# Cosformer attention into a quick-GELU MoE layer: two numerators of batch 0 in one PSUM tile, with early denominators and a different idle stream

## The chip, the cores and the metric

The kernel runs on one core of one Trainium2 chip. The metric is the device time of one execution in microseconds; 292.02 us is the median of three runs of the kernel before.

## The reference

Linear attention with cosine weights, for 8 batches, 8 heads, 576 positions and a head size of 64; then an expert layer over all 4608 tokens.

```python
def phi(x, c, s):
    r = np.maximum(x, 0.0)
    return np.concatenate([r * c, r * s], axis=-1)
q_p = phi(q, cos_w, sin_w)
k_p = phi(k, cos_w, sin_w)
kv = np.einsum('bhsf,bhsd->bhfd', k_p, v)
z = np.sum(k_p, axis=2)
num = np.einsum('bhsf,bhfd->bhsd', q_p, kv)
den = np.einsum('bhsf,bhf->bhs', q_p, z)[..., None] + 1e-06
return (num / den).astype(np.float32)
...
h = x @ w_in
g = h * (1.0 / (1.0 + np.exp(-1.702 * h)))
return (g @ w_out).astype(np.float32)
```

x is the attention's output with the heads side by side, 4608 x 512; w_in is 512 x 2048, w_out 2048 x 512.

## The kernel before

The order of the instructions on every engine is that of the source: the kernel is written under a manual schedule, and the framework only adds the waits. A wait is put where an instruction touches a tile that an instruction of another engine wrote or read.

Batch 0 has a lead-in of its own, since nothing can hide it. Its order on TensorE, with the lines of the profile:

- idle(12) (L346) multiplies a tile of zeros, warm, while the first loads run. Idle matmuls also stand between the next steps.
- trig (L140 on ScalarE, L142 on VectorE and for one slice on GpSimd) makes kr, the weighted relu of k, in nine slices j of 64 positions. ksum(j) (L218) multiplies each slice with sel, so that the PSUM tile z holds the sum over positions for each head; ksum_evac (L222) copies it to column 64 of kvs. The second half of k lands later than the first, so slices 3 to 8 come later.
- trig makes qn from q likewise; qturn_pe(c) (L171) transposes two slices of it at a time, a chunk c of 128 positions, and qevac(c) (L179 ScalarE, L181 VectorE) copies it to qT.
- kv_mm(0, 2) and kv_mm(2, 4) (L207) make kv for heads 0 to 3 and 4 to 7, and kv_evac (L212) copies each to columns 0 to 63 of kvs.
- den_early(0) (L244) makes the denominators of chunk 0 from column 64 of kvs alone, before kv is there; inv_of (L236, L238) adds 1e-6 and takes the reciprocal.
- num_mm(c) (L230) makes the numerators of chunk c, with 65 columns for a head so that the last is the denominator; num_div(c) (L254) multiplies with the reciprocal into xn; xturn_mm(c) (L274) transposes xn back into free columns of the same PSUM tile, and xturn_evac (L280, ScalarE) copies that into xT. Chunk 4 has 64 positions and goes through a DMA transpose (L285).
- part(c, ...) (mm1_part, L295) multiplies w_in with chunk c of xT for one of the first four slices of the hidden layer, so that the expert layer starts before all of xT is there. Then gelu (L300), the other slices, and mm2 (L332) with w_out.

Two PSUM pools matter. pmm has four tiles of one bank ("mm"): idle, z, the transposes of q, the early denominators and the hidden slices take them in turn. pat has two tiles of two banks ("at"): the two halves of kv, then one chunk's numerators after the other. So num_mm(2) takes the tile of chunk 0, and waits until xturn_evac(0, 0) has read it; num_mm(3) takes that of chunk 1.

Batches 1 to 7 are pipelined: their loads, trig, transposes and kv run beside the expert layer of the batch before.

Of the kernel before, what the change touches and what calls it, by code (L numbers as in the profile page):

```python
# [9 lines left out]
F32 = mybir.dt.float32  # L10
BF16 = mybir.dt.bfloat16
AF = mybir.ActivationFunctionType
MUL = mybir.AluOpType.mult
# [6 lines left out]
def kernel(  # L20
# [9 lines left out]
    nc = tc.nc  # L30
    B, H, S, D = q.shape
    d_model = H * D
    d_ff = moe_w_in.shape[1]
    KC = d_model // 128
# [3 lines left out]
    NI = H // 2  # L38

    const = ctx.enter_context(tc.tile_pool(name="const", bufs=1))  # L40
# [4 lines left out]
    small = ctx.enter_context(tc.tile_pool(name="small", bufs=3))  # L45
    pmm = ctx.enter_context(tc.tile_pool(name="pmm", bufs=4, space=PSUM))
    pat = ctx.enter_context(tc.tile_pool(name="pat", bufs=2, space=PSUM))
# [13 lines left out]
    for t, src, cut in ((kf, k, 192), (qf0, q, 256)):  # L61
# [9 lines left out]
    ident = const.tile([128, 128], BF16)  # L71
    nc.gpsimd.memset(ident, 1.0)
    nc.gpsimd.affine_select(out=ident, in_=ident, compare_op=mybir.AluOpType.is_equal,
                            fill=0.0, base=0, pattern=[[-1, 128]], channel_multiplier=1)
    warm = const.tile([128, 512], BF16)
    nc.vector.memset(warm, 0.0)
    pos_f = const.tile([128, NP], F32)
    nc.vector.tensor_copy(pos_f, pos_i)
    nc.vector.tensor_scalar(pos_f[64:128, 0:NS], pos_f[64:128, 0:NS], float(-S), None, op0=ADD)
# [2 lines left out]
    scale = math.pi / 2.0 / S  # L82
    halfpi = const.tile([128, 1], F32)
    nc.vector.memset(halfpi, math.pi / 2.0)
    sel = const.tile([128, 2], BF16)
    nc.vector.memset(sel, 0.0)
    for hh in range(2):
        nc.vector.memset(sel[hh * 64:hh * 64 + 64, hh:hh + 1], 1.0)
    nc.scalar.activation(sinw, pos_f, AF.Sin, scale=scale)
    nc.scalar.activation(cosw, pos_f, AF.Sin, scale=-scale, bias=halfpi)  # L90
    gl = const.tile([128, 1], F32)
# [8 lines left out]
    qT = one.tile([128, H, 640], BF16, name="qT")  # L100
# [66 lines left out]
    def qturn_pe(c, home=None):  # L167
        tp = pmm.tile([128, 2, NI, 128], BF16, name="mm") if home is None else home
        for j in range(2 * c, min(2 * c + 2, NS)):
            for i in range(NI):  # L170
                nc.tensor.transpose(tp[:, j % 2, i], qn0[:, j, i, :], ident)  # L171
        tps[c] = tp

    def qevac(c, act=False):
        n = min(2 * c + 2, NS) - 2 * c
        o = qT[:, :, ds(c * 128, n * 64)].rearrange("f h (j p) -> f j h p", j=n)
        i = tps.pop(c)[:, 0:n].rearrange("f j i (hh p) -> f j (i hh) p", hh=2)
        if act:
            nc.scalar.activation(o, i, AF.Copy)  # L179
        else:  # L180
            nc.vector.tensor_copy(o, i)  # L181
# [10 lines left out]
    st = {}  # L192

    def kv_open(i0=0, i1=NI):
        t = pat.tile([128, 2, 512], F32, name="at")
        for i in range(i0, i1):
            st["kv", i] = t[:, :, ds((i - i0) * 65, 65)]
        st["ps", i0] = t[:, :, 0:(i1 - i0) * 65]
        if i0 == 0:
            st["kvs"] = small.tile([128, 2, NI, VW], BF16, name="kvs", bufs=2)  # L200

    def kv_mm(i0, i1, rhs, col, n):
        for i in range(i0, i1):
            for j in range(NS):
                for hh in range(2):
                    r = slice(hh * 64, hh * 64 + 64)
                    nc.tensor.matmul(st["kv", i][:, hh, ds(col, n)], kr[r, j, i, :], rhs(r, i, j),  # L207
                                     start=(j == 0), stop=(j == NS - 1))

    def kv_evac(i0, i1, n=65):  # L210
        o = st["kvs"][:, :, i0:i1, 0:n]
        nc.vector.tensor_copy(o, st["ps", i0].rearrange("p hh (i e) -> p hh i e", e=65)[:, :, :, 0:n])  # L212

    def ksum(j):
        if j == 0:
            st["z"] = pmm.tile([128, NI, 2], F32, name="mm")
        for i in range(NI):
            nc.tensor.matmul(st["z"][:, i], kr[:, j, i, :], sel, start=(j == 0 and i == 0),  # L218
                             stop=(j == NS - 1 and i == NI - 1))

    def ksum_evac():
        nc.vector.tensor_copy(st["kvs"][:, :, :, 64], st["z"].rearrange("f i hh -> f hh i"))  # L222

    nums = {}

    def num_mm(c):
        ps = pat.tile([128, 2, 512], F32, name="at")
        for h in range(H):
            i, hh = divmod(h, 2)
            nc.tensor.matmul(ps[:, h // 4, ds((h % 4) * 65, 65)], qT[:, h, ts(c, 128)],  # L230
                             st["kvs"][:, hh, i, 0:65], start=True, stop=True)
        nums[c] = [ps]

    def inv_of(d):
        den = small.tile([128, 2, 4], F32, name="den")
        nc.vector.tensor_scalar(den, d, 1e-6, None, op0=ADD)  # L236
        inv = small.tile([128, 2, 4], F32, name="inv")
        nc.vector.reciprocal(inv, den)  # L238
        return inv

    def den_early(c):
        d = pmm.tile([128, 2, 4], F32, name="mm")
        for h in range(H):
            nc.tensor.matmul(d[:, h // 4, h % 4:h % 4 + 1], qT[:, h, ts(c, 128)],  # L244
                             st["kvs"][:, h % 2, h // 2, 64:65], start=True, stop=True)
        return inv_of(d)

    def num_div(c, inv=None):
        ps = nums[c][0]
        pv = ps[:, :, 0:260].rearrange("p a (h e) -> p a h e", h=4)  # L250
        if inv is None:
            inv = inv_of(pv[:, :, :, 64])
        xn = small.tile([128, 2, 4, 64], BF16, name="xn", bufs=4)
        nc.vector.tensor_tensor(xn, pv[:, :, :, 0:64],  # L254
                                inv.unsqueeze(3).to_broadcast([128, 2, 4, 64]), op=MUL)
        nums[c].append(xn)
# [6 lines left out]
    def x_open(b):  # L263
        x[b] = xpool.tile([128, KC, MT], BF16, name="xT")

    def x_of(b, c):
        return xt[:, :, ts(b, 64)] if c == 4 else x[b][:, :, ts(c, 128)]

    def xturn_mm(c):
        ps, xn = nums[c]  # L270
        xv = xn.rearrange("p a h e -> p (a h e)")
        for kc in range(KC):
            o = ps[:, kc // 2, ds(264 + (kc % 2) * 64, 64)].bitcast(BF16)
            nc.tensor.transpose(o, xv[:, ts(kc, 128)], ident)  # L274

    def xturn_evac(b, c):
        ps = nums.pop(c)[0]
        i = ps[:, :, 264:392].bitcast(BF16).rearrange("p a (k t) -> p a k t", k=2)
        o = x_of(b, c).rearrange("p (a k) t -> p a k t", a=2)
        nc.scalar.activation(o, i, AF.Copy)  # L280
# [10 lines left out]
    def mm1_part(b, fc, t0, t1):  # L291
        if t0 == 0:
            hp[fc] = pmm.tile([128, MT], F32, name="mm")
        for kc in range(KC):
            nc.tensor.matmul(hp[fc][:, t0:t1], w_in_of(kc, fc), x[b][:, kc, t0:t1],  # L295
                             start=(kc == 0), stop=(kc == KC - 1))
# [42 lines left out]
                eng = nc.sync if last else nc.gpsimd  # L339
                eng.dma_start(out=dst[:, c0:c1], in_=ysb[p0:p0 + n, c0:c1])  # L340

    def idle(n, w=None):
        if w is None:
            w = pmm.tile([128, 512], F32, name="mm")
        for _ in range(n):
            nc.tensor.matmul(w, warm[:, 0:128], warm, start=True, stop=True)  # L346
        return w

    def vb_rhs(r, i, j):
# [2 lines left out]
    def vt_rhs(r, i, j):  # L352
        return vt[r, j, i, 0:65]

    w = idle(12)
    for j in (0, 1):
        trig(kr, kf, j)
    for j in (2, 6, 7, 8):
# [2 lines left out]
        trig(kr, kf, j)  # L361
    kv_open(0, 2)
    kv_open(2, 4)
    for j in (0, 1, 2):
        ksum(j)
    for j in (3, 6, 4, 7, 5):
        idle(1, w)
        ksum(j)
    idle(1, w)
    ksum(8)  # L370
    for j in (0, 1):
        trig(qn0, qf0, j)
    ksum_evac()
    idle(1, w)
    qturn_pe(0)
# [15 lines left out]
    qevac(1)  # L391
    qevac(2, act=True)
    inv0 = den_early(0)
    kv_evac(0, 2, 64)
    kv_mm(2, 4, vb_rhs, 0, 64)
    kv_evac(2, 4, 64)
    qturn_pe(3)
    qevac(3, act=True)
    num_mm(0)
    num_div(0, inv0)  # L400
    num_mm(1)
    num_div(1)
    qturn_pe(4)
    qevac(4)
    idle(1)
    x_open(0)
    xturn_mm(0)
    xturn_evac(0, 0)
    num_mm(2)
    num_div(2)  # L410
    xturn_mm(1)
    xturn_evac(0, 1)

    def part(c, *fcs):
        for fc in fcs:
            mm1_part(0, fc, c * 128, c * 128 + 128)

    part(0, 0, 1, 2, 3)
    num_mm(3)
    num_div(3)  # L420
    xturn_mm(2)
    xturn_evac(0, 2)
    part(1, 0, 1, 2, 3)
    num_mm(4)
    num_div(4)
    xturn_mm(3)
# [156 lines left out]
```

## Time and profile before

| | |
|---|---|
| median of 3 runs | 292.02 us (291.79 to 292.14) |
| profiled execution | 292.75 us |
| its span | 291.0 us |
| TensorE busy | 281.8 us, 97% |
| VectorE busy | 123.7 us, 43% |
| ScalarE busy | 133.1 us, 46% |
| granted clock of TensorE | 1.0 |

The profile is of one execution. Its span runs from the first to the last instruction; the time of an execution has 1.75 us around that in this case. A matmul's duration in the records has the time through the array in it, so neighbours overlap: the pace of a row of matmuls is read from their starts. PE is TensorE's matmuls, PEld its weight loads, DVE VectorE, ACT ScalarE, POOL GpSimd, SP the queue of SyncE.

### The profile page before, as it was taken

The numbers are of one execution on the slowest core, as the hardware profiler recorded it, in microseconds if no ns is written. First come the engines' busy times: TensorE is split into PE (matmuls) and PEld (weight loads), VectorE is DVE, ScalarE is ACT, GpSimd is POOL, SyncE is SP. The second block draws the span as 40 slices with busy tenths as digits, with TensorE's granted clock in tenths as the row PEclk, the third lists the DMA queues.
The fourth block names the chain that finished last, engine by engine and source line by source line (L and its number), as shares of the span: only waits on it lengthen the run. The fifth ranks groups of instructions, "written<-read, shape, count | busy, mean of one in ns | idle before, by whom it ended". The sixth has DMA issues, their size and how long they took to land.

```text
span 291.0 us, 5656 instructions
## 1 busy us (share of the span) xinstructions
PE 281.8 (97%) x2247; PEld 153.0 (53%) x2282; DVE 123.7 (43%) x356; ACT 133.1 (46%) x232; POOL 37.8 (13%) x71
## 2 busy tenths in 40 slices
PE   6989999999999999999999999999999999999995
PEld 2685475555555555555455545554555455544444
DVE  3872656912657354826582567156624200000000
ACT  6857564793157214721463136412651176751111
POOL 6560042301210011001100110011000100002000
PEclk9999999999999999999999999999999999999999
DMA  7999999982699877989797579846952600002322
GB/s 239 247 213 289 368 247 362 239 193 76 128 271 260 219 131 260 289 184 147 221 314 198 96 203 346 222 102 159 373 94 72 119 36 1 0 2 44 84 90 72
DMA packets 67770, 52.48 MB, mean 180 GB/s; under 512 B 47968, under 2 KB 57952, under 8 KB 67744
## 3 DMA queue, kind: packets, MB, share of 16 engines
q1 hardware_dynamic: 60320, 32.52, 47.0%
q0 software_dynamic: 7424, 19.60, 23.9%
q8 instruction: 18, 0.29, 0.4%
q14 instruction: 8, 0.07, 0.1%
HBM read 36.70 MB, written 9.44 MB: 159 GB/s over the span
## 4 chain that ended last, share of the span: by engine, by line
PE 91%; DMA 3%; ACT 2%; DVE 1%; issue 1%; SPq 1%; ACTq 0%
PE mm L332 42%; PE mm L295 37%; PE mm L312 5%; PE at L230 3%; PE at L207 3%; DMA qf<-in_q_dram 3%; ACT g L300 1%; PE at L274 1%; DVE qn L142 1%; DVE qT L181 0%; PE at L171 0%; ACT qT L179 0%; SPq L62 0%; DVE xn L254 0%; ACT xT L280 0%
## 5 line engine op out<-in xcount | busy, mean ns | idle before, releaser
L332 PE MATMUL mm<-w_out_sb,g 128*128 128x512 bf16 (+1 forms) x506 | 116.7, 372 | 1.3 <-issue 0.2
L295 PE MATMUL mm<-xT,w_in 128*128 128x512 bf16 (+1 forms) x551 | 111.9, 360 | 0.5
L300 ACT ACTIVATE g<-mm 128x512 bf16<-128x512 f32 x128 | 75.6, 598 | 31.0 <-PE mm L295 31.0
L295 PEld LDWEIGHTS <-w_in 128*128 128x128 bf16 x560 | 59.8, 113 | 50.9
L332 PEld LDWEIGHTS <-g 128*128 128x128 bf16 x528 | 48.6, 98 | 49.1
L336 ACT ACTIVATE ysb<-mm 128x512 f32<-128x512 f32 (+1 forms) x37 | 21.7, 586 | 105.9 <-PE mm L332 103.0
L340 POOL DMA_DIRECT2D out_dram<-ysb x39 | 21.3, 547 | 204.7 <-ACT ysb L336 204.7
L142 DVE TENSOR_SCALAR kr<-kf,cosw 128x256 bf16<-128x256 f32 x64 | 22.6, 353 | 29.4 <-DMA kf<-in_k_dram 29.4
L254 DVE TENSOR_TENSOR xn<-at,inv 128x512 bf16<-128x512 f32 x40 | 27.7, 691 | 1.9 <-PE at L230 0.4
L142 DVE TENSOR_SCALAR kr<-kf,sinw 128x256 bf16<-128x256 f32 x64 | 22.2, 347 | 0.0
L212 DVE CAST kvs<-at 128x520 bf16<-128x520 f32 (+1 forms) x9 | 5.6, 634 | 33.7 <-PE at L207 33.7
L236 DVE TENSOR_SCALAR den<-at 128x8 f32<-128x8 f32 x39 | 6.5, 166 | 31.4 <-PE at L230 31.4
L230 PEld LDWEIGHTS <-qT 128*128 128x128 bf16 x320 | 14.8, 97 | 8.8 <-issue 0.8
L230 PE MATMUL at<-kvs,qT 128*128 128x65 bf16 x320 | 16.1, 193 | 0.7 <-ACT xT L280 0.7
L155 DVE TENSOR_SCALAR qn<-qf,sinw 128x512 bf16<-128x512 f32 (+1 forms) x30 | 14.4, 480 | 0.0
L155 DVE TENSOR_SCALAR qn<-qf,cosw 128x512 bf16<-128x512 f32 (+1 forms) x30 | 14.3, 476 | 0.0
L312 PE MATMUL mm<-xt,w_in 128*128 128x512 bf16 x63 | 13.9, 379 | 0.1
L332 PE MATMUL mm<-w_out_sb,gl_t 128*128 128x512 bf16 x63 | 13.9, 379 | 0.1
L313 ACT ACTIVATE gl_t<-mm 128x512 bf16<-128x512 f32 x16 | 9.6, 597 | 4.2 <-PE mm L312 4.2
L207 PEld LDWEIGHTS <-kr 64*128 64x128 bf16 x576 | 9.3, 94 | 2.8 <-issue 2.5
L312 PEld LDWEIGHTS <-w_in 128*128 128x128 bf16 x64 | 7.2, 113 | 6.6
L332 PEld LDWEIGHTS <-gl_t 128*128 128x128 bf16 x64 | 6.3, 98 | 7.5
(63 smaller groups left out, 114.5 us busy)
## 6 DMA issues: line engine op xcount, KB each, us to landing
kf<-in_k_dram SPq DMA_DIRECT2D x5, 1152.0 KB, 6.7
vf<-in_v_dram SPq DMA_DIRECT2D x5, 1152.0 KB, 9.5
qf<-in_q_dram SPq DMA_DIRECT2D x5, 1024.0 KB, 5.9
out_dram<-ysb POOLq DMA_DIRECT2D x20, 256.0 KB, 3.9
out_dram<-ysb POOLq DMA_DIRECT2D x19, 128.0 KB, 3.2
kf<-in_k_dram POOLq DMA_DIRECT2D x2, 1152.0 KB, 11.3
vf<-in_v_dram POOLq DMA_DIRECT2D x2, 1152.0 KB, 15.7
w_in<-in_moe_w_in_dram POOLq DMA_DIRECT2D x4, 512.0 KB, 9.5
```

What stands on the lines that cost most here:

```text
L142: eng.tensor_scalar(o, i, 0.0, w[:, j:j + 1], op0=MAX, op1=MUL)
L155: nc.vector.tensor_scalar(o, i, 0.0, sc, op0=MAX, op1=MUL)
L207: nc.tensor.matmul(st["kv", i][:, hh, ds(col, n)], kr[r, j, i, :], rhs(r, i, j), start=(j == 0), stop=(j == NS - 1))
L230: nc.tensor.matmul(ps[:, h // 4, ds((h % 4) * 65, 65)], qT[:, h, ts(c, 128)], st["kvs"][:, hh, i, 0:65], start=True, stop=True)
L254: nc.vector.tensor_tensor(xn, pv[:, :, :, 0:64], inv.unsqueeze(3).to_broadcast([128, 2, 4, 64]), op=MUL)
L295: nc.tensor.matmul(hp[fc][:, t0:t1], w_in_of(kc, fc), x[b][:, kc, t0:t1], start=(kc == 0), stop=(kc == KC - 1))
L300: nc.scalar.activation(g, hp.pop(fc), AF.Gelu_apprx_sigmoid)
L312: nc.tensor.matmul(hps, w_in_of(kc, fc), xt[:, kc, :], start=(kc == 0), stop=(kc == KC - 1))
L313: nc.scalar.activation(gl_t[:, fc, :], hps, AF.Gelu_apprx_sigmoid)
L332: nc.tensor.matmul(yp[t, c0][:, c0:c1], w, w_out_sb[:, fc, c0:c1], start=(fc == 0), stop=(fc == FC - 1))
L336: nc.scalar.activation(ysb[:, c0:c1], yp[t, c0][:, c0:c1], AF.Identity)
L340: eng.dma_start(out=dst[:, c0:c1], in_=ysb[p0:p0 + n, c0:c1])
```

## The change

Only batch 0's lead-in changes.

- The opening stream of 12 bf16 idle matmuls becomes two in fp32 and three in bf16, on one smaller tile of zeros that is read four times over. The six idle matmuls between the k sums go, and idle(1) after chunk 4's transposes.
- sel has 64 equal columns for each head in place of one, so each ksum matmul streams 128 columns, and z fills a bank.
- den_early is called for chunk 1 as well, after kv's second half; both chunks' denominators share a PSUM tile.
- The numerators of chunks 0 and 1 go to one pat tile, n1, chunk c in bank c, 64 columns for a head. Their transposes are written back to the first half of the same bank.
- num_mm(2) takes the other pat tile, that of kv's second half, and stands right behind the numerators of chunk 1.
- part(1, 0) is moved in front of xturn_mm(2).

```diff
-    warm = const.tile([128, 512], BF16)
-    nc.vector.memset(warm, 0.0)
+    warm32 = const.tile([128, 128], F32)
+    nc.vector.memset(warm32, 0.0)
+    warm = warm32.bitcast(BF16)
...
-    sel = const.tile([128, 2], BF16)
+    sel = const.tile([128, 2, 64], BF16)
...
-            st["z"] = pmm.tile([128, NI, 2], F32, name="mm")
+            st["z"] = pmm.tile([128, NI, 2, 64], F32, name="mm")
...
     def den_early(c):
-        d = pmm.tile([128, 2, 4], F32, name="mm")
+        if c == 0:
+            st["den"] = pmm.tile([128, 2, 2, 4], F32, name="mm")
+        d = st["den"][:, c]
...
+    def num1_mm(c):
+        if c == 0:
+            st["n1"] = pat.tile([128, 2, 512], F32, name="at")
+        for h in range(H):
+            nc.tensor.matmul(st["n1"][:, c, ts(h, 64)], qT[:, h, ts(c, 128)],
+                             st["kvs"][:, h % 2, h // 2, 0:64], start=True, stop=True)
+
+    def num1_div(c, inv):
+        xn = small.tile([128, 2, 4, 64], BF16, name="xn", bufs=4)
+        nc.vector.tensor_tensor(xn, st["n1"][:, c].rearrange("p (a h e) -> p a h e", a=2, h=4),
+                                inv.unsqueeze(3).to_broadcast([128, 2, 4, 64]), op=MUL)
+        nums[c] = xn
+
+    def x1turn_mm(c):
+        xv = nums.pop(c).rearrange("p a h e -> p (a h e)")
+        for kc in range(KC):
+            nc.tensor.transpose(st["n1"][:, c, ts(kc, 64)].bitcast(BF16), xv[:, ts(kc, 128)], ident)
+
+    def x1turn_evac(b, c):
+        i = st["n1"][:, c, 0:256].bitcast(BF16).rearrange("p (k t) -> p k t", k=KC)
+        nc.scalar.activation(x_of(b, c), i, AF.Copy)
...
-    w = idle(12)
+    w = idle(2, t=warm32)
+    idle(3, w)
...
-    for j in (0, 1, 2):
+    for j in (0, 1, 2, 3, 6, 4, 7, 5, 8):
         ksum(j)
-    for j in (3, 6, 4, 7, 5):
-        idle(1, w)
-        ksum(j)
-    idle(1, w)
-    ksum(8)
...
+    inv1 = den_early(1)
     qturn_pe(3)
     qevac(3, act=True)
-    num_mm(0)
-    num_div(0, inv0)
-    num_mm(1)
-    num_div(1)
+    num1_mm(0)
+    num1_mm(1)
+    num1_div(0, inv0)
+    num1_div(1, inv1)
+    num_mm(2)
     qturn_pe(4)
     qevac(4)
-    idle(1)
+    num_div(2)
     x_open(0)
-    xturn_mm(0)
-    xturn_evac(0, 0)
-    num_mm(2)
-    num_div(2)
-    xturn_mm(1)
-    xturn_evac(0, 1)
+    x1turn_mm(0)
+    x1turn_evac(0, 0)
+    x1turn_mm(1)
+    x1turn_evac(0, 1)
...
     num_mm(3)
     num_div(3)
+    part(1, 0)
     xturn_mm(2)
     xturn_evac(0, 2)
-    part(1, 0, 1, 2, 3)
+    part(1, 1, 2, 3)
```

More of the change, by code (lines that the diff above doesn't have):

```diff
@@ L84 @@
     nc.vector.memset(halfpi, math.pi / 2.0)
-    sel = const.tile([128, 2], BF16)
+    sel = const.tile([128, 2, 64], BF16)
     nc.vector.memset(sel, 0.0)
     for hh in range(2):
-        nc.vector.memset(sel[hh * 64:hh * 64 + 64, hh:hh + 1], 1.0)
+        nc.vector.memset(sel[hh * 64:hh * 64 + 64, hh], 1.0)
     nc.scalar.activation(sinw, pos_f, AF.Sin, scale=scale)
@@ L221, in ksum_evac @@
     def ksum_evac():
-        nc.vector.tensor_copy(st["kvs"][:, :, :, 64], st["z"].rearrange("f i hh -> f hh i"))
+        nc.vector.tensor_copy(st["kvs"][:, :, :, 64], st["z"][:, :, :, 0].rearrange("f i hh -> f hh i"))
     nums = {}
@@ L340, in mm2, with idle @@
                 eng.dma_start(out=dst[:, c0:c1], in_=ysb[p0:p0 + n, c0:c1])
-    def idle(n, w=None):
+    def idle(n, w=None, t=warm):
         if w is None:
@@ L345, in idle @@
         for _ in range(n):
-            nc.tensor.matmul(w, warm[:, 0:128], warm, start=True, stop=True)
+            nc.tensor.matmul(w, t[:, 0:128], t[:, 0:128].unsqueeze(1).to_broadcast([128, 4, 128]),
+                             start=True, stop=True)
         return w
```

## The prediction

> **What bounds the kernel now.** The page comes first. TensorE holds the span and the chain that ended last is nearly all TensorE, so what the change can win or lose is the time at which TensorE reaches its unbroken run of w_in and w_out matmuls.
>
> ```profile
> PE 281.8 (97%) x2247; PEld 153.0 (53%) x2282; DVE 123.7 (43%) x356; ACT 133.1 (46%) x232; POOL 37.8 (13%) x71
> ```
>
> The busy times by stretch say where TensorE is not full. The columns are the stretch, its length, and the busy time of PE, PEld, DVE, ACT and POOL, then the granted clock and DMA.
>
> ```profile
> 14.20:16.51 2.31, 1.30 (x29) 1.07 (x27) 1.87 (x6) 1.62 (x2) 2.31 (x4) 1.00 1.25 209
> 16.51:19.73 3.22, 3.22 (x69) 3.22 (x69) 2.38 (x8) 1.19 (x2) 2.22 (x4) 1.00 1.24 205
> ...
> 52.00:291.00 239.00, 234.16 (x1682) 122.82 (x1709) 93.32 (x262) 99.36 (x171) 18.39 (x34) 1.00 0.65 158
> ```
>
> From 16.51 on TensorE has almost no hole; after 22 us its list of waits has one entry, 0.2 us of issue. A shift of the start of that run therefore goes to the end nearly whole. The chain of waits up to 17 us (start, length, what) shows what sets that start:
>
> ```profile
> 2.39 8.26 DMA qf<-in_q_dram
> 10.67 1.51 DVE qn L142 x4
> ...
> 13.18 0.64 PE at L207 x36
> 13.82 0.55 PE mm L171 x8
> 14.38 0.28 PE at L230 x8
> ...
> 14.68 0.70 DVE xn L254
> ...
> 15.42 0.41 PE at L274 x4
> ...
> 15.86 0.61 ACT xT L280
> ...
> 16.51 0.40 PE at L230 x8
> ```
>
> It begins with the landing of the second half of q at 10.65, which the change does not touch. Then come kv's second half (13.18), the transposes of q's chunk 3 (13.82), chunk 0's numerator (14.38), its division on VectorE (14.68), its transposes (15.42), their copy to xT on ScalarE (15.86 to 16.46), and at 16.51 num_mm(2), which waits for that copy to free its PSUM tile.
>
> **Before 13.8 us: no cost.** The 12 opening idle matmuls become two fp32 and three bf16 ones, the six between the k sums go, and each k sum matmul streams 128 columns for 2.
>
> ```profile
> 1.25 4.20 PE L346 MATMUL mm<-warm 128*128 128x512 bf16 x12 [1.25 <-DVE warm L76]
> 7.46 0.25 PE L218 MATMUL mm<-sel,kr 128*128 128x2 bf16 x4 [1.05 <-DVE kr L142]
> ```
>
> The first k sum waits for kr (DVE ready near 5.05) and the fourth for the second half of k, at 7.46, after 1.05 us of idle TensorE. An fp32 matmul has no row in this trace. The low bound for the five is five cold bf16 ones at 0.42 us (spacing of the first opening loads): 2.1 us, an end at 3.2. For a high bound I take as much as twelve cold ones: 5.0 us, an end at 6.2. The first 12 k sums then need 12 x 0.057 = 0.7 us (0.057 is a 128-column matmul of L295: 16 from 16.97 to 17.86) and are through by 6.9, ahead of 7.46. At either end nothing is late; below nothing is excluded because q's landing is next on the path. The Trainium skill ("FP8 and Floating Point Precision", TensorE Precision Notes) gives true fp32 four passes; by it the stream would end near 5.5, inside the same bounds. The last k sums wait for ScalarE's kr at 9.3; 4 x 0.057 = 0.23 us replace four short ones and one idle matmul (0.10 + 0.22), so the transposes of q start where they did. Memsets of sel grow on a VectorE that idles 2.3 us to 4.43.
>
> **The new den_early(1).** It goes in front of the transposes of chunk 3, on the chain: the same eight matmuls for chunk 0 took 12.83 to 13.11, 0.28 us. Its two VectorE steps (0.19 + 0.12 us start to start, from 13.29, 13.48, 13.60) follow kv_evac at 14.22 and end before the numerators do: hidden, with 0.5 us to spare.
>
> **Numerators 0 and 1 in one tile.** Both now sit in one two-bank tile n1, and the built program's waits go by tile, not by bank. num1_div(0) waits for the last matmul of chunk 1. x1turn_mm(0) waits for num1_div(1), since that read the tile. x1turn_mm(1) waits for ScalarE's x1turn_evac(0,0). In the kernel before, each chunk had its own tile and none of these waits was there. Step by step:
> - kv's second half is issued by 13.76; den_early(1) +0.28, chunk 3's transposes +0.45 (13.76 to 14.21): the numerators start at 14.49 against 14.21.
> - Sixteen numerator matmuls at 0.23 to 0.27 us for eight (16.51 to 16.74, 17.86 to 18.13), then 0.17 us until the last has ended: 15.12 to 15.20. The 0.09 us that they waited for kv_evac at 14.30 are gone, which is in these times.
> - num1_div(0) starts 0.03 later, 15.15 to 15.23, against 14.68. num1_div(1) follows 0.60 us behind (a division to the next step on VectorE, 14.68 to 15.28) and takes 0.69, so it ends at 16.44 to 16.52. The second division hardly moves, but chunk 0's transposes now stand behind it and not behind the first. In the timeline of before they start while the second division has not begun:
>
> ```profile
> 15.42 0.40 PE L274 MATMUL at<-ident,xn 128*128 128x128 bf16 x4 [0.32 <-DVE xn L254]
> ...
> 15.71 0.69 DVE L254 TENSOR_TENSOR xn<-at,inv 128x512 bf16<-128x512 f32 x1
> ```
>
> - So x1turn_mm(0) starts at 16.49 to 16.57 against 15.42, 1.07 to 1.15 late. The copy starts 0.44 behind (15.42 to 15.86), takes 0.60, and 0.05 on TensorE goes on: 17.58 to 17.66 against 16.51, now with x1turn_mm(1). Queued behind that on TensorE are the 16 matmuls of part(0) and all that follows.
>
> **num_mm(2) moved ahead, xturn_mm(2) moved back.** From that point to the first matmul of part(3) took 16.51 to 20.58, 4.07 us. After it is: x1turn_mm(1) 0.23, part(0) 0.89, num_mm(3) 0.27, part(1, 0) 0.23; then xturn_mm(2) to num_mm(4), which waits for the copy of chunk 2: 1.08 (18.13 to 19.16, and 0.05), where only 0.23 + 12 x 0.057 = 0.91 of TensorE work lies, so 0.17 us of new idle; num_mm(4) 0.24; xturn_mm(3) to part(3) 1.08 as now (19.50 to 20.58, bounded by that copy). Sum 4.02. The 0.23 us of num_mm(2) that are saved are nearly given back, because four matmuls fewer cover chunk 2's copy. num_mm(2), chunk 4's transposes, qevac(4) and chunk 2's division (done near 17.9, needed at 19.2) hide in the wait for the first copy; so does the idle(1) that is dropped. The later PSUM slots are free long before: hp[3] waits for qevac(4), done near 16.85, needed at 18.5. SP's transpose of chunk 4 and the gelus move with the rest.
>
> **Sum.** +1.11 (the middle of 1.07 to 1.15) - 0.05 = +1.06 us. If den_early(1) costs only 0.20 (its rows start 12.83 to 13.00), 0.08 less; if single-bank numerators or their division go slower by a tenth (16 x 0.03 and 2 x 0.69), 0.18 more; faster by as much, 0.18 less. So +0.8 to +1.3. The span becomes 291.0 + 1.06 = 292.06; the profiled execution was 292.75, 1.75 over its span and 0.73 above the median of 292.02, so I put the sum on the median: 293.08, and 292.8 to 293.3 for this case with nothing else.
>
> **Rivals.**
> 1. The waits on n1 do not bite, as if each bank were a tile of its own. Then division 0 needs only chunk 0: start 14.94, transposes at 15.68, copy to 16.72, chunk 1's transposes already done in its shadow, part(0) at 16.77, and with 0.89 + 0.27 + 0.23 + 1.08 + 0.24 + 1.08 part(3) starts at 20.56 against 20.58: 292.0, no change. It decides wherever x1turn_mm(0) starts before num1_div(1) ends. Against it stand the waits in the built program; for it, that the two chunks share no address. The Trainium skill ("PSUM — Partial Sum Buffer", PSUM bank collisions raise a hardware error) asks for a guard by bank and quadrant, not by address; chunk 0 and chunk 1 are in different banks, so by that rule the waits are needless. It would allow rival 1's time, but the chip only executes the waits that are there. Chance 0.05.
> 2. The delay is swallowed later: TensorE in batch 1 stands behind something tied to a landing and not to TensorE. The place would be qturn_pe(0) at 37.88, whose q lands at 34.84. It needs 1.06 us of such waiting. Against it: VectorE has made its first slices by 35.9, and TensorE idles 0.2 us in all of the later list of waits. It would give 292.1 to 292.4. Chance 0.04.
> 3. TensorE's clock falls to its cold pace before 14 us. The opening matmuls show both paces: loads 0.42 us apart at first, then four in 0.75 us. If fp32 matmuls go like bf16 ones (the low bound), the stream ends at 3.2 with nothing until 5.1, and from there a doubled pace on the chain costs 0.28 + 0.45 + 0.5 (den_early, transposes, numerators) plus up to 0.6 on kv: 1 to 2 us more, 294.1 to 295.1. For it: of 18 idle matmuls up to the last k sum 5 are left, and TensorE would idle some 1.5 us there instead of 1.05. Against it: the k sums now stream 36 x 128 columns, 2.05 us of work for the 6 x 0.21 they replace, and after the 1.05 us gap the transposes at 9.68 still ran at 0.056 us each. The Trainium skill ("TensorE: Matmul & The Clock Gate", The HAM clock gate) puts the fall behind an idle window of about 3.4 us; no gap here comes near, so by that rule the clock holds. Chance 0.06.
> 4. The front of the chain comes earlier, with q's landing no longer last. Nothing in the change touches a transfer before 14.8. Chance 0.03, perhaps 0.3 us faster.
>
> **Numbers.** The forecast has 0.82. Its own range, with 0.2 us of spread between runs (291.79 to 292.14 before), is 292.6 to 293.5; I go to 292.6 to 293.8 for the part of rival 3 where only a few matmuls run cold. About 0.2% (0.6 us) is what a measurement of this kernel tells from no change. Faster: rival 4 and a little of 1: 0.04. Same: most of rivals 1 and 2: 0.07. Slower: 0.89.
>
> **What would show it.** In the profile after, chunk 0's transposes should start behind the second division, not the first, near 16.5; the two copies to xT should stand more than a microsecond apart with the first from about 16.97; TensorE should idle about 0.9 us before x1turn_mm(0), 0.7 us before x1turn_mm(1) and 0.17 us before num_mm(4); part(3) should start near 21.6, and batches 1 to 7 keep their lengths. I am wrong if x1turn_mm(0) starts before the second division ends, if the delay at 20.6 is not found again at the end, or if the transposes at 9.7 run at 0.1 us each.

## The result and the profile after

The changed kernel takes 292.9 us (median of 9 runs, 292.77 to 293.43) against 292.02 us for the kernel before in the same session (9 runs, 291.5 to 292.52): a ratio of 1.0036, interval [1.0025, 1.0047]. The forecast was 293.1. In the profile, though, the two spans are equal, 291.0 us each, and the profiled executions took 292.77 and 292.75 us. That contradiction has to be solved first, and it is solved by not looking at absolute times.

The shares of the engines on the page have not moved (TensorE 97% as before). The busy times by stretch of the kernel after, for two of the stretches that the prediction shows:

```profile
14.20:16.51 2.31, 0.82 (x16) 0.62 (x12) 2.23 (x6) 1.10 (x2) 2.31 (x4) 1.00 1.25 208
...
52.00:291.00 239.00, 234.15 (x1682) 122.82 (x1709) 93.31 (x262) 99.34 (x171) 18.13 (x34) 1.00 0.62 159
```

TensorE's busy time from 14.20 to 16.51 has fallen from 1.30 to 0.82 us: a hole that was not there. The rest of the kernel, from 52 us on, is the same to 0.01 us. So time was lost near 15 us and must have been won ahead of it. The chain that ended last of the kernel after says where (start, length, what):

```profile
1.31 4.95 DMA kf<-in_k_dram
...
6.28 1.58 DVE kr L143 x4
...
10.86 0.71 PE at L208 x36
...
12.95 0.28 PE mm L247 x8
13.23 0.47 PE mm L172 x8
13.70 0.48 PE at L255 x16
...
14.21 1.30 DVE xn L260 x2
...
15.55 0.40 PE at L267 x4
...
15.97 0.61 ACT xT L271
...
16.62 0.38 PE at L267 x4
...
20.59 1.49 PE mm L320 x21
```

From kv on it is the forecast chain: den_early(1) (L247), the transposes of chunk 3 (L172), sixteen numerators (L255), both divisions (L260), only then the transposes (L267), one copy to xT, the second transposes, and part(3) at 20.59. But ahead of kv it does not begin with q: it goes through the landing of k and TensorE's own work. The first matmul of kv_mm(0, 2) stands at 10.86 here and stood at 11.38 in the profile of before. In that execution VectorE took its first step on q's second half at 10.67; here it did at 9.65. The profiled execution of before had a late q, by luck, and was with 292.75 us above all nine timed runs of its kernel.

The list of TensorE's waits of the kernel after (what waited, for what: us, times, longest) has the two new waits:

```profile
PE at L267 <- DVE xn L260: 0.9, 1, 0.9
PE at L267 <- ACT xT L271: 0.7, 1, 0.7
```

The front of the kernel differs from one execution to the next, while what lies behind part(3) is fixed: its first matmul to the span's end is 270.4 to 270.5 us in every profile of this study. So I compare the kernels by one interval, from the first matmul of kv_mm(0, 2) to the first of part(3), and by timed runs.

### The profile page after: what moved, and what is told of

Same layout as the page of the kernel before. It is cut to its first block, busy times and chain, and to the rows that moved or that the text cites. A ratio compares the mean times of both kernels' runs of the same rounds, so it can differ in the third digit from the quotient of the medians.

```text
span 291.0 us, 5648 instructions
## 1 busy us (share of the span) xinstructions
PE 282.3 (97%) x2245; PEld 153.9 (53%) x2278; DVE 123.8 (43%) x356; ACT 133.1 (46%) x232; POOL 37.7 (13%) x71
## 4 chain that ended last, share of the span: by engine, by line
PE 93%; ACT 2%; DMA 2%; DVE 1%; issue 1%; SPq 0%; ACTq 0%
PE mm L357 42%; PE mm L320 37%; PE mm L337 5%; PE at L208 3%; PE at L231 3%; DMA kf<-in_k_dram 2%; ACT g L325 1%; PE mm L172 1%; DVE kr L143 1%; PE at L299 0%; PE mm L219 0%; DVE xn L260 0%; PE at L172 0%; ACT qT L180 0%; PE at L267 0%
## 5 line engine op out<-in xcount | busy, mean ns | idle before, releaser
L279 DVE TENSOR_TENSOR xn<-at,inv 128x512 bf16<-128x512 f32 x38 | 26.3, 691 | 1.3
L231 PEld LDWEIGHTS <-qT 128*128 128x128 bf16 x304 | 14.1, 97 | 8.2
L231 PE MATMUL at<-kvs,qT 128*128 128x65 bf16 x304 | 15.4, 193 | 0.0
```

Of the source, the lines that this page charges most:

```text
L279: nc.vector.tensor_tensor(xn, pv[:, :, :, 0:64], inv.unsqueeze(3).to_broadcast([128, 2, 4, 64]), op=MUL)
```

## The experiments

The theory: the lost time is the two waits that the shared tile n1 makes, about 1.06 us, from which the rest of the change gives a little back. The rivals: the loss sits in the new front (fp32 idle matmuls, wide k sums), or the order of part(1) makes it, or the equal spans are right and nothing was lost. All ratios below are to the kernel before, run on the same chip in the same session.

### Two tiles for n1

```diff
         if c == 0:
-            st["n1"] = pat.tile([128, 2, 512], F32, name="at")
+            st["n1", 0] = pat.tile([128, 2, 512], F32, name="at")[:, 0]
+        else:
+            st["n1", 1] = pmm.tile([128, 512], F32, name="mm")
```

The PSUM tile for the transposes of chunk 4 is taken ahead of num1_mm(1), so that the pool's turn still works out. All else is as in the kernel after.

> The changed kernel, but chunk 1's numerators in a one-bank tile of the other pool, so that no wait ties chunk 1 to chunk 0. Theory (the loss is the three waits on the shared tile n1): division 0 starts 0.2 us earlier, chunk 0's transposes stand behind division 0 and not behind division 1, part(0) starts 1.03 us earlier than in the changed kernel, counted from the landing of q; the time falls by about 1.0 us, to that of the kernel before, ratio to it 0.999 to 1.001. Rival F (the loss is in the front: fp32 idle matmuls, wide k sums, fewer idle matmuls): the time stays 0.9 to 1.1 us above the kernel before, ratio 1.003 to 1.004. Rival L (the loss is only in when the loads land, and the later part is no slower): also no gain over the changed kernel.

It took 291.96 us (12 runs), ratio 1.0001 [0.9993, 1.001]: the loss is gone. In the list of TensorE's waits of this kernel for 9 to 22 us, one entry is left where there were two:

```profile
PE mm L269 <- DVE xn L262: 0.2, 1, 0.2
```

Its chain that ended last:

```profile
11.08 0.71 PE at L208 x36
...
14.20 0.70 DVE xn L262
...
14.95 0.41 PE at L269 x4
...
15.38 0.61 ACT xT L273
...
16.03 1.05 PE mm L322 x16
...
19.77 1.49 PE mm L322 x21
```

The transposes start behind one division (0.70 us, not 1.30), and the first copy to xT is followed at once by w_in's matmuls. From kv to part(3): 19.77 - 11.08 = 8.69 us, against 20.59 - 10.86 = 9.73 after. The waits on the shared tile are worth 1.04 us; beside the tile only the moment at which that PSUM tile for chunk 4 is taken was changed.

### The front alone, and the back alone

The first kernel is the kernel before with the new idle stream and the wide k sums; the second is the kernel after with the old ones.

```diff
-    w = idle(12)
+    w = idle(2, t=warm32)
+    idle(3, w)
...
-    sel = const.tile([128, 2], BF16)
+    sel = const.tile([128, 2, 64], BF16)
```

> The kernel before with only the new front: two fp32 and three bf16 idle matmuls, no idle matmul between the k sums, 128-column k sums. Numerators, denominators and transposes as before. Theory (shared tile): no more than 0.15 us from the kernel before, ratio 0.9995 to 1.0008. Rival F: the whole loss is here, +0.9 to +1.1 us, ratio 1.003 to 1.004.

> The changed kernel with the front of the kernel before: 12 idle matmuls, idle matmuls between the k sums, 2-column k sums; shared tile n1, early denominators and the moved part(1, 0) stay. Theory (shared tile): +0.9 to +1.1 us on the kernel before, ratio 1.003 to 1.004, with chunk 0's transposes behind division 1. Rival F: no difference from the kernel before.

The front alone: 292.02 us (11 runs), ratio 1.0003 [0.9994, 1.0012], no difference that the interval could tell. The back alone: 292.58 us (11 runs), ratio 1.0022 [1.0013, 1.003]; the same kernel once more in a later session, with the kernel after beside it:

> The back half alone once more, beside the changed kernel. Theory (shared tile alone): the same time as the changed kernel within 0.15 us. If the first value (ratio 1.0022) holds: 0.65 us above the kernel before, and 0.2 to 0.4 us under the changed kernel.

> The changed kernel beside its back half alone on one chip. Theory (shared tile alone): both kernels 0.9 us above the kernel before, ratio 1.0028 to 1.0034, and 9.7 to 9.8 us from the first kv matmul to part(3) in both profiles. If the new front adds a loss of its own: this kernel 0.2 us or more above the back half alone, with the first kv matmul later by as much.

The back alone gave 292.59 us, 1.0026 [1.0015, 1.0037], the kernel after 292.96 us, 1.0033 [1.0021, 1.0046]. The chain that ended last of the back alone (first session) has the same steps from kv on as the kernel after, and a third beginning, the landing of v:

```profile
4.53 6.37 DMA vb<-in_v_dram
...
10.94 0.71 PE at L207 x36
...
14.34 1.30 DVE xn L259 x2
...
20.71 1.49 PE mm L319 x21
```

20.71 - 10.94 = 9.77 us, against 9.73 in the kernel after. The front alone has 8.82. So most of the loss goes with the back half of the change. Two expectations were missed, though: the back alone stays under the 1.003 to 1.004 expected, and is 0.37 us under the kernel after where 0.15 was expected at most; the second reading put on record with it, 0.2 to 0.4 us under, came true. The part on the front below comes back to that.

### The two kernels profiled again

> The kernel before once more, for a second profile. If only the landing of q made its first profile late (first step on the second half of q at 10.67, against 9.6 to 10.0 in the other profiles), then here the landing is near 9.8, part(3) starts 9.9 to 10.05 us after it, and the time is 291.9 us. If the first profile's 10.67 is a property of the kernel before, it comes again.

> The changed kernel once more, on the chip and in the rounds of the kernel before. Theory (shared tile, 1.0 us from the landing of q to part(3)): +0.8 to +1.1 us, ratio 1.0027 to 1.0038; part(3) starts 10.9 to 11.0 us after the landing. If its effect is no more than the back half alone gave, ratio 1.0022.

The kernel before: 291.95 us against 291.78 for itself, 1.0005 [0.9993, 1.0018]. The kernel after: 293.0 us, 1.0041 [1.0026, 1.0055]. Now the spans differ, 289.9 and 291.1 us. The second profile of the kernel before, its chain:

```profile
1.30 4.83 DMA kf<-in_k_dram
...
6.16 2.51 ACT kr L140 x6
...
10.71 0.67 PE at L207 x36
...
19.52 1.49 PE mm L295 x21
```

q is not in it. VectorE's first step on q's second half, in the timeline of that profile, stands 1.2 us earlier than in the first:

```profile
9.46 0.35 DVE L142 TENSOR_SCALAR qn<-qf,cosw 128x256 bf16<-128x256 f32 x1
```

The interval from the first matmul of kv_mm(0, 2) (10.67 for this profile by the timeline) to the first of part(3), for all profiles:

| kernels | kv to part(3), us | profiles |
|---|---|---|
| old back (before again, front alone, and "before without three idles" below) | 8.82 to 8.87 | 3 |
| before, first profile, q late | 9.20 | 1 |
| shared n1 (after three times, back alone twice, two short openings below) | 9.71 to 9.77 | 7 |
| two tiles (the kernel above, and two below) | 8.60 to 8.69 | 3 |

The first profile of before is out of line since its q came so late that VectorE was still making qn while TensorE was at kv, and den_early(0) then waited for it. With the usual 8.85, the loss is 9.74 - 8.85 = 0.89 us; the timed runs gave +0.88, +1.22 and +1.03 by medians for the kernel after, +0.69 and +0.66 for the back alone. 0.89 us is a ratio of 1.0030, which lies in four of these five intervals and at the upper end of the fifth, the back alone's [1.0013, 1.003].

### The order of part(1)

The two-tile kernel with the old order:

```diff
-    part(1, 0)
     xturn_mm(2)
     xturn_evac(0, 2)
-    part(1, 1, 2, 3)
+    part(1, 0, 1, 2, 3)
```

> As the run with two tiles, and xturn_mm(2) ahead of all of part(1) again. Theory: the 0.17 us that TensorE idles ahead of num_mm(4) go, and num_mm(2) is saved from the chain for good: 0.15 to 0.2 us under the two-tile run, 1.2 us under the changed kernel, 0.1 to 0.3 us under the kernel before, ratio to it 0.999 to 1.000. If chunk 2's division is late instead, xturn_mm(2) waits for it and the gain is gone. Rival F: still 0.7 us or more above the kernel before.

291.81 us (11 runs), 0.9995 [0.9987, 1.0004]; kv to part(3) 8.63. The order is worth 0.06 us in the trace. By medians the run is 0.15 us under the two-tile run, but the two intervals overlap.

### The opening stream

In the kernel after, the five opening matmuls all in bf16, and one alone:

```diff
-    w = idle(2, t=warm32)
-    idle(3, w)
+    w = idle(5)
```

> The changed kernel with five bf16 matmuls in place of two fp32 and three bf16: the low bound of the prediction. The stream ends near 3.2 us and TensorE has nothing until 5.0. Theory (k sums warm the clock in time, the front has slack): time within 0.3 us of the changed kernel. Rival C (the clock stays cold): the k sums and the first transposes run at 0.107 us each, kv and numerators partly too, 1 to 2 us slower than the changed kernel.

> The changed kernel with one bf16 idle matmul in place of the opening stream, so TensorE is idle from 1.6 us to the first k sum near 5. Same reading as the run before, more strongly: if the opening stream is what warms the clock, matmuls run at half pace until 3 to 4 us of work have passed, and the time is 1 to 2 us above the changed kernel; if the k sums alone do it before 10 us, it is within 0.3 us.

They took 293.47 us (4 runs, 1.0054 [1.0036, 1.0072]) and 293.77 us (4 runs, 1.0059 [1.0041, 1.0078]); the kernel after beside them had 293.0 (292.8 to 293.62, 6 runs). The runs of the first overlap with it; those of the second (293.5 to 294.03) nearly do not. The timeline of the one with a single opening matmul, TensorE:

```profile
7.23 2.74 PE L219 MATMUL mm<-sel,kr 128*128 128x128 bf16 x24 [0.51 <-DVE kr L143]
...
10.18 1.06 PE L172 MATMUL mm<-ident,qn 128*128 128x128 bf16 x8
11.04 0.67 PE L371 MATMUL mm<-warm 128*128 128x512 bf16 x2
```

The eight transposes start 10.18 and the next idle matmul 11.04: 0.107 us each, where the kernel after does eight in 0.44 us (9.29 to 9.73 in its timeline), 0.055 each. So TensorE's pace was half up to 11 us, the 24 k sums took 2.74 us, and kv starts at 12.09 instead of 10.86. Kv to part(3) is 9.71: warm again, and the same loss. The five bf16 matmuls are less clear: their profiled execution also had v and q late (vb on the chain to 12.27, VectorE's first step on q at 11.02), so its 12.31 for kv is not the opening's doing alone.

### Without three idle matmuls

The two-tile kernel with the old order, and the kernel before, each without the three idle matmuls behind the last k sum:

```diff
     ksum_evac()
-    idle(1, w)
...
-    idle(2, w)
     qturn_pe(1)
```

> Two tiles, xturn_mm(2) ahead of part(1), and without the three idle matmuls between the last k sum and the second transposes of q. Where k's second half lands as in the later profiles, TensorE is full from 8.8 us to kv, so these idle matmuls are on the path and not only cover: kv's first half 0.2 us earlier (the second transposes then wait for ScalarE's slice of q), 0.15 us from the order of part(1), ratio to the kernel before 0.998 to 0.9995. If vb or q land last, or the clock drops, nothing or a loss: 1.000 to 1.003.

> The kernel before without the same three idle matmuls (after the last k sum). If the front is bound by TensorE from the last k sum on: 0.2 us faster, ratio 0.9985 to 0.9998. If the landing of q binds, as the prediction had it: no change, 0.9995 to 1.0005. If the clock needs them: slower.

291.87 us (1.0002 [0.9993, 1.0011]) and 292.05 us (1.0007 [0.9998, 1.0016]): nothing, where 0.998 to 0.9995 was expected of the first. What the idle matmuls leave free is waiting. In the first, the second transposes wait 0.33 us for ScalarE's qn, and in the second kv waits 0.38 us for vb. No version here is measurably faster than the kernel before. Two tiles under the old front were not run.

## Why the prediction was right, and where it was not

**The waits on n1: right.** In the timeline of the kernel after, in both places the idle time in brackets and what ended it are the forecast ones:

```profile
15.55 0.38 PE L267 MATMUL at<-ident,xn 128*128 128x128 bf16 x4 [0.92 <-DVE xn L260]
...
16.62 0.38 PE L267 MATMUL at<-ident,xn 128*128 128x128 bf16 x4 [0.69 <-ACT xT L271]
```

Forecast 0.9 and 0.7 us of idle time, measured 0.92 and 0.69. From x1turn_mm(0) to x1turn_mm(1) it is 16.62 - 15.55 = 1.07 us (1.09 in the sum). Rival 1 is refuted: the two-tile kernel keeps the two chunks in different banks as the kernel after does, and is 1.04 us shorter from kv to part(3), so it is the waits on the shared tile that cost. The Trainium skill ("PSUM — Partial Sum Buffer", PSUM bank collisions raise a hardware error) wants a guard by bank and quadrant; the two-tile kernel has no guard between the banks of chunks 0 and 1, so it agrees with that rule, and the kernel after guards more than the rule asks for.

**The terms, from the start of kv_mm(2, 4)** (13.12 in the first profile of before, 12.24 after, in the timeline):
- den_early(1): 12.88 to 13.10, 0.22 us. The sum took 0.28, which in the first profile ran to the next weight load, that of kv at 13.11; the alternative of 0.20 was nearer.
- sixteen numerators 13.54 to 14.01: 0.47 us, inside the 0.46 to 0.54 of the working.
- x1turn_mm(0): 15.42 - 13.12 = 2.30 before, 15.55 - 12.24 = 3.31 after, +1.01; the sum took +1.11. den_early's 0.06 is in that, the rest in the numerators.
- x1turn_mm(0) to what follows the first copy: 16.51 - 15.42 = 1.09 before, 16.62 - 15.55 = 1.07 after, -0.02; the sum had it unchanged.
- from there to part(3): 20.58 - 16.51 = 4.07 before, 20.59 - 16.62 = 3.97 after, -0.10; the sum took -0.05. The expected wait of 0.17 us ahead of num_mm(4) is there: xturn_mm(2) to num_mm(4) takes 18.20 to 19.28, 1.08 us, as forecast. That this wait comes from moving part(1, 0) was half right: with it moved back, only 0.06 us return.
- together +1.01 - 0.02 - 0.10 = +0.89 against a sum of +1.06, and inside its +0.8 to +1.3.

**What the change gives back.** The two-tile kernel is 8.85 - 8.69 = 0.16 us shorter than the old back from kv to part(3): that is all that the rest of the back half (denominators from k's sums, no copy in front of num_mm(2)) is worth. 1.04 lost, 0.16 won.

**"Before 13.8 us: no cost": only partly.** The fp32 stream in this execution, in the timeline and then in that of TensorE's weight loads:

```profile
1.11 4.69 PE L371 MATMUL mm<-warm 128*128 128x512 f32 x7 [1.11 <-DVE warm L76]
...
2.12 0.34 PEld L371 LDWEIGHTS mm<-warm 128*128 128x128 f32 x1 [0.52 <-issue]
2.98 0.34 PEld L371 LDWEIGHTS mm<-warm 128*128 128x128 f32 x1 [0.52 <-issue]
```

Five matmuls are seven records: an fp32 one is two, each 0.86 us long by the spacing of the loads, so 1.7 us for one matmul. That is four times the 0.42 us of a cold bf16 one and agrees with the four passes of the Trainium skill ("FP8 and Floating Point Precision", TensorE Precision Notes). The stream let the first k sum start at 5.64, and in the other profiles with it at 5.15 to 5.97, inside the bounds of the prediction; eleven slow passes of 0.42 us from 1.11 would end at 5.7, so its 5.5 was a little short. In the second profile of the kernel after the first twelve k sums stood about 0.107 us apart (5.96 to 7.13), not 0.057, and yet the transposes start 3.01 us behind the step on k's second half there as in the first (9.41 - 6.40 and 9.29 - 6.28). But "at either end nothing is late" was wrong for the low end. With the five in bf16, or with one, TensorE was not yet at its full pace when the k sums and transposes came, and the single-matmul opening cost 0.77 us by medians. I had costed that as rival 3, for gaps in the stream; what these two change is how much TensorE does before 5 us. In the kernel after the transposes at 9.29 run at 0.055 us, and rival 3 did not happen in it. "No cost" fails in a second way, through the landing of k, which is the point on the front below.

**"Its start is q's landing": true of one execution only.** This is a step that failed, beside that of no cost in the front. I read the chain of one profile as the kernel's chain. In the others VectorE's first step on q's second half is at 9.37 to 10.37 (11.02 in the opening with five bf16 matmuls), and the front ends with k's landing and ScalarE's kr, with TensorE's own queue, or with v's landing, all within a few tenths of a microsecond. So the absolute marks that I gave (first copy 16.97, part(3) 21.6, span 292.06) were all about 1 us late: 15.97, 20.59, 291.0. The forecast survived since the sum was of intervals and was put on the median of the timed runs. The profiled 292.75 us, 0.73 above that median, was the hint that something in this execution was unusual, and I had noted it without asking what.

**Swallowed later (rival 2): no.** The shift goes to the end whole (270.4 to 270.5 us behind part(3)'s start in every profile).

**The new front costs a few tenths of its own.** The prediction put the front at nothing and said under rival 4 that nothing in the change touches a transfer before 14.8. The interval of the front alone, 1.0003 [0.9994, 1.0012], can't tell a cost. But its fastest run, 291.90 us, is slower than 19 of the 35 runs of the kernel before beside it. The fastest runs of each session tell the parts better, since late landings lengthen some of the others (292.75 us with a late q, 293.57 with a late v). The lowest of the kernel before is 291.49 to 291.56 in every session; the front alone lies 0.39 us above it, the back alone 0.93 and 0.96, the kernel after 1.27 to 1.33.

The traces show a place for some of it. VectorE's first step on the second half of k follows its first step on the first half by 2.02 to 2.06 us in all nine profiles with the new front (two of them with a shorter opening), and by 1.84 to 1.88 in four of five with the old one (2.36 in the first profile of before). In the seven profiles whose chain goes through k's landing and not through a slow pace, v or q, kv starts 4.51 to 4.59 us after that step on the second half, whichever the front. So about 0.2 us of the front's cost is k landing later. Why it does, and where the rest is, stays open.

So it is in part luck that 1.06 us lies amid the medians of +0.88 to +1.22: the back half gave 0.89, less than the sum, and the front added what the sum had at nothing.

## What to carry to other kernels

Two halves of a PSUM tile that are written, read and overwritten at different times are one thing to waits that go by tile: here that put 1.04 us on the path, and giving each bank its own tile took it away. Compare two profiles by the interval between two events that both have, on the path, and not by span; and where a profiled execution lies outside the timed runs, suspect that its input landings are untypical. A stage in which several landings and engines finish within a few tenths of a microsecond, as this front, gave nothing back when only one of them was eased.

## What the runs showed of the hardware

**The pace of TensorE rises at different moments.** The same twelve bf16 matmuls opened two kernels; the timeline of the second profile of before, and of the back alone:

```profile
1.25 4.25 PE L346 MATMUL mm<-warm 128*128 128x512 bf16 x12 [1.25 <-DVE warm L76]
```

```profile
1.25 5.30 PE L370 MATMUL mm<-warm 128*128 128x512 bf16 x12 [1.25 <-DVE warm L76]
```

In the first, eight start about 0.43 us apart and the ninth at 4.47, 3.2 us after the first; the last four are 0.22 us apart, twice the pace. In the second all twelve are slow, for over 5 us. The Trainium skill ("TensorE: Matmul & The Clock Gate", The HAM clock gate) gives about 3.4 us of time from cold to full pace and says that the moment varies by 0.5 us either way with the start; the first agrees with that, the second lies outside. The granted clock reads 1.00 in all these stretches, the slow ones too, so the pace has to be read from the starts of the matmuls. In neither of the two does the chain that ended last go through the opening stream: in the first it goes through k's landing and ScalarE's kr, in the second through v's landing at 10.90.

**Transfers were slower with the new front.** The busy times by stretch, 6 to 8 us, of the second profiles of before and after (the last column is GB/s):

```profile
6.00:8.00 2.00, 1.30 (x19) 0.64 (x17) 1.84 (x6) 1.84 (x5) 1.58 (x3) 1.00 1.08 391
```

```profile
6.00:8.00 2.00, 1.91 (x21) 1.62 (x19) 1.60 (x5) 1.60 (x4) 1.60 (x3) 1.00 1.08 352
```

Every profile with the old front has 385 to 391 GB/s there, every one with the new front 332 to 355. TensorE's load alone does not explain it, since the back alone keeps TensorE busy for all of the 2.00 us at 391 GB/s. From 4 to 6 us, ahead of the landing of k's second half, it is 394 to 396 GB/s with the old front (373 in the first profile of before) and 368 to 385 with the new one. The fp32 matmuls are not needed for it, since the two openings without them have 332 and 354 GB/s from 6 to 8 us. The wide k sums, the wider sel and the idle matmuls that are gone were not tried apart.
